# A fused attention and two-expert-layer kernel: dense chunks in the order 0, 6, 1, 7, …, sums of the output weights made in the dense blocks, and loads, splits and fetches of the output stage begun elsewhere

## The chip, the core and the metric

The kernel runs on one core of one Trainium2 chip. The metric is the device time of one launch in microseconds (us), taken as the median of several runs. All traces come from one profiled execution each.

## What is computed

Three layers follow one another; each works on the result of the one before. The reference, cut to its arithmetic:

```python
# attention: batch 4, 8 heads, 576 positions, 64 features, local mask or strided mask by head
x = softmax(mask(q @ k.T / 8)) @ v                    # -> 2304 tokens x 512
# dense layer: w_gate, w_val are 512 x 1536, w_out is 1536 x 512
x = (1 / (1 + exp(-(x @ w_gate)))) * (x @ w_val) @ w_out
# routed layer: w1 is 8 x 512 x 1024, w2 is 8 x 1024 x 512
do = (x @ w_skip) > 0
e  = argmax(x[do] @ w_gate2);  g = softmax(...)[e]
x[do] += g * (relu(x[do] @ w1[e]) @ w2[e])
```

The precision asked for is that of float32. The kernel splits an operand into a high part (a cast on ScalarE, to the matmul's float32r type) and a low part (the operand minus the high part, on VectorE), and forms each product from three matmuls (lines 563 to 565: high by high, high by low, low by high).

## The kernel before

**Stages.** Attention takes 0 to 138 us of the profiled execution, the dense blocks (gate and value products) 138 to 398, the output stage (the product with w_out) 398 to 576, and the routed experts the rest.

**Dense blocks.** The 1536 hidden features are 12 chunks f of 128; the tokens are three pairs p of two tiles of 384. `Block(f, p)` computes gate and value of one chunk for one pair by a Strassen-Winograd scheme of seven products (A11, A12, A22, S1 to S4 by B11, B21, B22, T1 to T4). `period` interleaves a block with the end of the block before, 42 matmuls of 384 columns, about 7.28 us. A block passes four PSUM tiles: psA, psB, psC and psD; ScalarE copies psB to psC (line 602, `onto`) before the products S4·B22 and A22·T4 of the block before are added to it. ACT is in order, so a copy stands behind whatever cast was queued ahead of it.

**Hidden results.** The gated result of a block goes to DRAM (`gts`) in the form in which the output stage wants it: seven operands B11, B21, B22 and T1 to T4 again. A chunk of the first half ("low") writes plain tiles with SP's queue; a chunk of the second half ("high") adds its own onto T2, T3 and T4 with accumulating DMAs from POOL's queue, and writes B21 and B22. With chunks in the order 0 to 11, all accumulations lie in the second half of the dense stage.

**Output weights.** w_out arrives as pairs of 32-bit words and is converted on DVE (`convert`, jobs of `background`) into 128 x 512 floats, stored with one DMA a chunk (line 556) to `wos`. The output stage loads quarters of it, makes the sums S1 to S4 (`sums_w`, lines 972 to 975, 12 DVE instructions of 128x512), stores three of them (`wss`, POOL's queue) and loads them again (line 948, SP).

**Output stage.** It has NSTEP = 63 steps k, 21 for each pair p: products P1 (k = 0 to 2 of a pair), P2, P6, P7, P5, P4, P3, three steps each, one for each group g of two chunks. A step has 12 matmuls. It needs an operand tile xt[k] (loaded from `gts`, line 938 or 941, five steps ahead, split by ACT at line 958 and DVE at line 966 two or three steps ahead) and a weight tile (wtA… for A11, A12, A22; wtS… for the sums; loaded at lines 948 and 951, split by `w_halves`). `finish` takes a finished pair of sums out of PSUM, splits it, and hands it to `turn_back`, whose narrow matmuls (lines 1075 and 1076) turn the result back to token rows and make the router's scores beside it; they run in small pieces between the products.

**What sets the order.** Instructions stand on each engine's queue in the order in which the program is written: the step loop runs a table `side` of actions by step (`at(k, …)`), and a list `after_act` of DVE work that is to follow ACT's. SP's DMA queue is in order, too: a DMA whose tile is still read, or whose source is still written, holds all that stand behind it. Moreover a DMA of SP waits for the one eight places ahead of it, since a ring of eight semaphores serves them.

**Places that the change touches.** The end of the dense stage, where A11 and xt2 are loaded at the start of block (11, 1) and xt0, xt1 and A12_0 at the start of (11, 2), while A12_1, A12_2, xt3 and xt4 follow the dense stage; the first 20 steps (`w_loads`, `sums_w`); `finish` at the change from one pair to the next; and the last steps, in which `fetch_head` (line 1193) fetches rows of expert 0's tokens from `xs`, a DRAM table that a scatter fills just before.

Of the kernel before, what the change touches and what calls it, by code (L numbers as in the profile page):

```python
# [23 lines left out]
def kernel(  # L24
# [51 lines left out]
    NG = NC // 4  # L76

# [23 lines left out]
    wos = [[dram.tile([128, 2, DM], F32, name=f"wo{h}_{g}") for g in range(NG)] for h in range(2)]  # L101
    wss = {(nm, g): dram.tile([128, 2, 256], F32, name=f"ws{nm}_{g}") for nm in ("S1", "S3", "S4") for g in range(NG)}

# [336 lines left out]
    def fetch_w(f, nm):  # L440
        raw = raw_of[f, nm] = raw_w([128, 4, 128, 2], I32, f"w{nm}{f}")
        if nm == "o":
            src = moe_w_out.bitcast(I32)[128 * f:128 * f + 128, :]
            nc.sync.dma_start(raw.rearrange("p c n t -> p (c n t)"), src)
        else:
            src = (moe_w_gate if nm == "g" else moe_w_val).bitcast(I32)[:, 256 * f:256 * f + 256]
            nc.sync.dma_start(raw.rearrange("p c n t -> p c (n t)"), src.rearrange("(c p) f -> p c f", p=128))
# [98 lines left out]

    def out_weights(f, follow=None):
        box = []

        def dst():  # L550
            if not box:
                box.append(part_x(f"wof{f}").rearrange("p a n -> p (a n)")[:, 0:DM])
            return box[0]

        def store():
            nc.sync.dma_start(wos[f // (NC // 2)][f % (NC // 2) // 2][:, f % 2, :], box[0])
# [3 lines left out]
        wo_jobs[f] = convert(f, "o", dst, store)  # L560
# [10 lines left out]
    class Block:  # L571
# [39 lines left out]
        def put(self, op, t, add=False):  # L611
            dst = gts[self.p, op, self.f % (NC // 2) // 2][:, self.f % 2, :]
# [5 lines left out]
        def store(self, nm, by, i):  # L618
# [4 lines left out]
            x, y, low = self.tm[nm], self.tm[by], self.f < NC // 2  # L623
# [232 lines left out]

    raws_left = []
    for f in range(2, NC):
        raws_left += [(f, "g"), (f, "v")] + ([(f - 3, "o")] if f > 2 else [])
    raws_left += [(f, "o") for f in range(NC - 3, NC)]  # L860
    outs_of = {f: [f - 2] for f in range(2, NC)}
    outs_of[NC - 2].append(NC - 3)
    outs_of[NC - 1] = [NC - 2, NC - 1]
# [50 lines left out]
    sum2 = []  # L914
    wt = {nm: [] for _, nm, _, _ in PROD}
    WHERE = {"A11": (0, 0), "A21": (0, 1), "A12": (1, 0), "A22": (1, 1)}
# [26 lines left out]
    def load_w(nm, g, of=None):  # L943

        if len(wt[nm]) <= g:
            wt[nm].append(slab([128, 2, 2, 256], F32, f"wt{nm}{g}"))
        if of == nm and nm[0] == "S":
            nc.sync.dma_start(wt[nm][g][:, 1], wss[nm, g])
        elif of:
            h, d = WHERE[of]  # L950
# [787 lines left out]
```

## Time and profile before

| | us |
|---|---|
| median of 3 runs | 771.02 |
| the runs | 770.71, 771.02, 773.42 |
| the profiled execution, its own time | 772.05 |
| its span (first to last instruction) | 770.3 |
| TensorE (PE) busy in the span | 719.8 (93%) |
| VectorE (DVE) busy | 561.1 (73%) |
| ScalarE (ACT) busy | 453.3 (59%) |
| GpSimd (POOL) busy | 258.1 (34%) |
| DMA traffic | 160.15 MB, mean 208 GB/s |

The busy share of PE is not a measure of its speed: matmuls are pipelined, and at a lower granted clock the same matmul counts as longer busy time. What PE could save is read from the time between two of its matmuls against their number. The pace of full clock stands in the dense blocks, where PE is busy throughout.

### The profile page before, as it was taken

The page shows a single profiled execution, that of the slowest core. Times are in us where ns is not written, and L with a number is a line of the kernel's source. Part 1 is how long each engine was busy: PE and PEld are TensorE (multiplying, and loading weights), DVE is VectorE, ACT ScalarE, POOL GpSimd, SP SyncE. Part 2 cuts the span into 40 slices and gives each one's busy share as a digit, 9 for nine tenths or more (in the row PEclk, how much of TensorE's full clock was granted, in tenths as well). Part 3 has the DMA queues.
Part 4 walks back from the last instruction along what each step waited for, and adds up shares of the span by engine and source line. Part 5 has one row for each costly group of instructions (what it writes and reads, how often), then busy time and mean ns, then how long its engine had stood idle before and what let it go on. Part 6 is the DMA issues. An engine that isn't in the chain of part 4 may idle for free.

```text
span 770.3 us, 14529 instructions
## 1 busy us (share of the span) xinstructions
PE 719.8 (93%) x4783; PEld 671.5 (87%) x4785; DVE 561.1 (73%) x1234; ACT 453.3 (59%) x1206; POOL 258.1 (34%) x296
## 2 busy tenths in 40 slices
PE   8999989999999999999976898999988999999994
PEld 5766667999999999999975798999977899999992
DVE  4799997988898888889654765657756756666760
ACT  5888885755455555555432655546654476767740
POOL 6677875000000043333331100210305355555510
PEclk9999999999999999999987898999999999999998
DMA  9999511466666699999989894786737677778720
GB/s 195 235 215 207 135 33 48 157 216 231 212 221 211 231 215 224 214 222 213 230 193 373 312 361 137 250 249 241 271 106 266 207 228 226 234 228 249 239 69 14
DMA packets 136555, 160.15 MB, mean 208 GB/s; under 512 B 60271, under 2 KB 104815, under 8 KB 136473
## 3 DMA queue, kind: packets, MB, share of 16 engines
q1 hardware_dynamic: 121208, 134.25, 56.7%
q0 software_dynamic: 12496, 21.49, 13.3%
q10 hardware_dynamic: 2768, 3.41, 1.2%
q8 instruction: 40, 0.66, 0.3%
q14 instruction: 43, 0.34, 0.1%
HBM read 105.07 MB, written 59.65 MB: 214 GB/s over the span
## 4 chain that ended last, share of the span: by engine, by line
PE 70%; DMA 9%; DVE 8%; ACT 5%; issue 3%; POOL 3%; SPq 1%; POOLq 0%; DVEq 0%; ACTq 0%
PE psZ L1524 5%; PE psB L564 5%; PE psB L565 5%; PE psB L563 5%; PE psA L563 4%; PE psA L565 4%; PE psD L565 4%; PE psD L563 4%; PE psA L564 4%; PE psD L564 4%; PE psX L1460 3%; PE psY L1460 2%; DMA xt<-gB 2%; DMA wtA<-wo 2%; POOL sm L313 2%
## 5 line engine op out<-in xcount | busy, mean ns | idle before, releaser
L614 POOL DMA_DIRECT2D gT<-sC x36 | 31.7, 1026 | 193.2 <-DVE sC L628 192.9
L958 ACT CAST xt<-xt 128x768 fp32r<-128x768 f32 (+1 forms) x74 | 53.6, 742 | 35.5 <-DMA xt<-gB 18.6
L966 DVE TENSOR_TENSOR xt<-xt 128x768 fp32r<-128x768 f32 (+1 forms) x74 | 60.4, 832 | 15.9 <-ACT xt L958 15.8
L300 ACT ACTIVATE sm<-psX,mx 96x128 f32<-96x128 f32 (+2 forms) x176 | 62.2, 378 | 9.8 <-DVE mx L294 7.8
L313 POOL TENSOR_TENSOR sm<-sm,rs 96x384 f32<-96x384 f32 (+2 forms) x64 | 55.5, 885 | 31.0 <-DVE rs L307 18.1
L609 DVE TENSOR_TENSOR u<-psD,u 128x384 f32<-128x384 f32 x70 | 38.7, 553 | 26.8 <-PE psD L565 26.7
L565 PE MATMUL psA<-xhB,wl 128*128 128x384 f32 x140 | 47.0, 336 | 1.3 <-DVE wl L536 1.3
L565 PE MATMUL psD<-xhT,wl 128*128 128x384 f32 x140 | 47.3, 338 | 0.3 <-DVE wl L536 0.3
L563 PE MATMUL psD<-xhT,wh 128*128 128x384 f32 x140 | 47.2, 337 | 0.0
L564 PE MATMUL psD<-xlT,wh 128*128 128x384 f32 x140 | 47.1, 337 | 0.0
L563 PE MATMUL psB<-xhT,wh 128*128 128x384 f32 x140 | 46.9, 335 | 0.0
L564 PE MATMUL psA<-xlB,wh 128*128 128x384 f32 x140 | 46.8, 334 | 0.0
L565 PE MATMUL psB<-xhT,wl 128*128 128x384 f32 x140 | 46.8, 334 | 0.0
L563 PE MATMUL psA<-xhB,wh 128*128 128x384 f32 x140 | 46.8, 334 | 0.0
L564 PE MATMUL psB<-xlT,wh 128*128 128x384 f32 x140 | 46.8, 334 | 0.0
L564 PE MATMUL psB<-xt,wtS 128*128 128x384 f32 x108 | 39.2, 363 | 4.1 <-DVE xt L966 4.1
L563 PE MATMUL psB<-xt,wtS 128*128 128x384 f32 x108 | 39.2, 363 | 3.2 <-ACT xt L958 1.8
L602 ACT COPY psC<-psB 128x384 f32<-128x384 f32 x35 | 16.3, 466 | 43.1 <-PE psB L565 43.1
L595 ACT COPY u<-psB 128x384 f32<-128x384 f32 x70 | 34.0, 485 | 12.7 <-PE psB L565 12.0
L1505 POOL DMA_INDIRECT out_dram<-xg x16 | 15.3, 956 | 77.4 <-DVE xg L1504 66.4
L565 PE MATMUL psB<-xt,wtS 128*128 128x384 f32 x108 | 39.1, 362 | 1.9 <-DVE wtS L1277 1.9
L300 ACT ACTIVATION_READ_ACCUMULATOR sm<-psX,mx 96x1 f32 (+2 forms) x176 | 38.7, 220 | 0.0
(786 smaller groups left out, 2536.5 us busy)
## 6 DMA issues: line engine op xcount, KB each, us to landing
w1r<-in_moe_w_dram SPq DMA_DIRECT2D x28, 512.0 KB
w2r<-in_moe_w_dram SPq DMA_DIRECT2D x28, 512.0 KB
xt<-gT SPq DMA_DIRECT2D x30, 384.0 KB
gT<-u SPq DMA_DIRECT2D x54, 192.0 KB
xt<-gB SPq DMA_DIRECT2D x22, 384.0 KB
gT<-sC POOLq DMA_DIRECT2D x36, 192.0 KB
gB<-sA SPq DMA_DIRECT2D x33, 192.0 KB
wg<-in_moe_w_gate_dram SPq DMA_DIRECT2D x12, 512.0 KB
```

Source lines behind the costliest of these rows:

```text
L300: nc.scalar.activation(sm[:n, w, 0:c], src[:, w, :], AF.Exp, bias=mx[:n, w:w + 1], accum_out=sums[:n, h, w:w + 1])
L313: nc.gpsimd.tensor_tensor(x, x, rs[:n, h, 0:m].rearrange("p (w o) -> p w o", o=1).to_broadcast([n, m, c]), op=ALU.mult)
L563: nc.tensor.matmul(ps, lhsT=whi, rhs=xhi, start=start, stop=False, skip_group_check=skip)
L564: nc.tensor.matmul(ps, lhsT=whi, rhs=xlo, start=False, stop=False, skip_group_check=skip)
L565: nc.tensor.matmul(ps, lhsT=wlo, rhs=xhi, start=False, stop=stop, skip_group_check=skip)
L595: nc.scalar.copy(self.tm[nm], self.ps["B"])
L609: nc.vector.tensor_tensor(self.tm[nm], self.ps["D"], self.tm[nm], op=ALU.add)
L614: nc.gpsimd.dma_start(dst, t, accum_op=ALU.add)
L958: nc.scalar.copy(h.bitcast(F32R), l)
L966: nc.vector.tensor_tensor(l.bitcast(F32R), l, h, op=ALU.subtract)
L1460: nc.tensor.matmul(ph, lhsT=w[kk][0][:, fs], rhs=xk, start=(kk == 0), stop=(kk == KD - 1))
L1524: nc.tensor.matmul(py, lhsT=w2h, rhs=h, start=(f == 0), stop=(f == NF - 1))
```

## The change

The chunks of the dense stage are taken in the order 0, 6, 1, 7, …, so that every second chunk is a low one and every second a high one. When a high chunk's w_out is converted, both halves for the group are there: four more DVE jobs make S1 to S4 of the chunk pair in place (128x256 each, 24 instructions in all) and SP stores the seven ready tiles (42 stores of 128 KB, in place of 12 of 256 KB). `sums_w`, `w_loads` and the table `wss` are gone; the output stage loads ready tiles with `load_w`.

A11, xt2, xt0, xt1 and A12_0 are all loaded at the start of block (11, 1), and their splits are jobs from the start of (11, 2). Behind the dense stage POOL loads S2_2, and SP A12_1, A12_2, S2_0, xt3 and xt4. The later weight tiles are loaded four steps ahead.

`finish` is cut up: sums that are added first (line 1238) are added at once, their casts follow one step later and the low parts behind them; others have the casts at once and the low parts in `after_act`. In the last four steps its tiles come from the pool of the operand tiles. Pieces of `turn_back` move by one to two steps. `fetch_head` moves from SP's queue to POOL's, one step later, and the loads of expert 0's weights (`load_e0`) by up to two steps.

```diff
+    CHUNK = [i // 2 + NC // 2 * (i % 2) for i in range(NC)]
...
-            src = moe_w_out.bitcast(I32)[128 * f:128 * f + 128, :]
+            src = moe_w_out.bitcast(I32)[128 * CHUNK[f]:128 * CHUNK[f] + 128, :]
...
         def store():
-            nc.sync.dma_start(wos[f // (NC // 2)][f % (NC // 2) // 2][:, f % 2, :], box[0])
+            for nm, a in ((("A12", 0), ("A22", 256)) if f % 2 else (("A11", 0),)):
+                put(nm, box(f)[:, a:a + 256])
...
+        j = convert(f, "o", lambda: box(f)[:, 0:DM], store)
+        if f % 2:
+            def sums(nm):
+                low, high = boxes[f - 1], boxes[f]
+                a11, a21, s1 = (low[:, 256 * i:256 * i + 256] for i in range(3))
+                a12, a22, s2 = (high[:, 256 * i:256 * i + 256] for i in range(3))
+                sub = nc.vector.scalar_tensor_tensor
+                if nm == "S1":
+                    sub(s1, in0=a21, scalar=-1.0, in1=a22, op0=ALU.mult, op1=ALU.subtract)
+                    put(nm, s1)
...
+                if nm == "S4":
+                    nc.vector.tensor_tensor(a11, a12, s2, op=ALU.subtract)
+                    put(nm, a11)
+            for nm in ("S1", "S2", "S3", "S4"):
+                j = Job("D", 0.4, lambda nm=nm: sums(nm), [j])
+        wo_jobs[f] = j
...
-            x, y, low = self.tm[nm], self.tm[by], self.f < NC // 2
+            x, y, low = self.tm[nm], self.tm[by], self.f % 2 == 0
...
-        if (f, p) == (NC - 1, NP - 1):
+        if (f, p) == (NC - 1, 1):
             for i in outs_of[f]:
                 need(wo_jobs[i])
-            for n in range(2):
+            for g in range(NG):
+                load_w("A11", g)
+            for n in (2, 0, 1):
                 load_x(n)
-            load_w("A12", 0, "A12")
-        if (f, p) == (NC - 1, 1):
-            for g in range(NG):
-                load_w("A11", g, "A11")
-            load_x(2)
+            load_w("A12", 0)
...
-    def finish(u, a, sums, adds=None):
-        sh, sl = (raw_w([128, 2, UT], F32R, f"s{n}{u}{a}") for n in "hl")
+    def finish(u, a, sums, k, adds=None):
+        if k < NSTEP - 4:
+            sh, sl = (raw_w([128, 2, UT], F32R, f"s{n}{u}{a}") for n in "hl")
+        else:
+            both = slab2([128, 2, 2, UT], F32R, f"s{u}{a}")
+            sh, sl = both[:, 0], both[:, 1]
...
+        if adds:
+            for c in range(2):
+                nc.vector.tensor_tensor(adds[c], adds[c], sums[c], op=ALU.add)
+            at(k + 1, do(lambda: (highs(adds), after_act.append(lambda: lows(adds)))))
+        else:
+            highs(sums)
+            if k + 1 < NSTEP:
+                after_act.append(lambda: lows(sums))
+            else:
+                lows(sums)
...
+    load_w("S2", 2, eng=nc.gpsimd)
+    for nm, g in (("A12", 1), ("A12", 2), ("S2", 0)):
+        load_w(nm, g)
     load_x(3)
-    for g in (1, 2):
-        load_w("A12", g, "A12")
     load_x(4)
-    w_loads(0)
-    at(0, do(lambda: w_loads(1)))
-    at(1, do(lambda: w_loads(2)))
...
-        xg, ins = fetch(0, PARTS[:1])
+        xg, ins = fetch(0, PARTS[:1], eng=nc.gpsimd)
...
-    at(NSTEP - 9, do(fetch_head))
+    at(NSTEP - 8, do(fetch_head))
```

On SP's queue at the end of the dense stage (wtA11g are the tiles of A11, wtA12g of A12, wtS2g of S2, each by group g; xt00 and xt01 are the halves of xt0) these rows stand in a row before; the store of the last converted chunk, wo1_2, is amid them:

```order
L938 DMA xt20_5007<-gB11_02_73 128x384
L938 DMA xt21_5008<-gB11_02_73 128x384
L556 DMA wo1_2_139<-wof11_4965 128x512
L938 DMA xt00_5082<-gB11_00_71 128x384
L938 DMA xt01_5083<-gB11_00_71 128x384
L938 DMA xt10_5086<-gB11_01_72 128x384
L938 DMA xt11_5087<-gB11_01_72 128x384
L951 DMA wtA120_5090<-wo1_0_137 128x2x256
L941 DMA xt3_5229<-gB21_00_74 128x768
L951 DMA wtA121_5212<-wo1_1_138 128x2x256
L951 DMA wtA122_5213<-wo1_2_139 128x2x256
L941 DMA xt4_5233<-gB21_01_75 128x768
```

and these after:

```order
L967 DMA xt20_5069<-gB11_02_73 128x384
L967 DMA xt21_5070<-gB11_02_73 128x384
L967 DMA xt00_5073<-gB11_00_71 128x384
L967 DMA xt01_5074<-gB11_00_71 128x384
L967 DMA xt10_5077<-gB11_01_72 128x384
L967 DMA xt11_5078<-gB11_01_72 128x384
L977 DMA wtA120_5081<-wA12_0_137 128x512
L977 DMA wtA121_5273<-wA12_1_138 128x512
L977 DMA wtA122_5274<-wA12_2_139 128x512
L977 DMA wtS20_5275<-wS2_0_146 128x512
L970 DMA xt3_5293<-gB21_00_74 128x768
L970 DMA xt4_5295<-gB21_01_75 128x768
```

The store of the last weights has moved ahead of all these loads, A12 and S2_0 stand ahead of xt3, and xt4 stands right behind xt3.

On ACT at the same place (ACTIVATE is a gate; the last row, a copy to psC, is what the PE needs for the last products of the dense stage) these stand before:

```order
L602 COPY psB_5112<-psA_5092 128x384
L958 CAST xt20_5007<-xt20_5007 128x384
L958 CAST xt21_5008<-xt21_5008 128x384
L606 ACTIVATE sC_111_5132<-psC_5099 128x384
L595 COPY u2_112_5140<-psB_5112 128x384
L606 ACTIVATE sA_112_5152<-psA_5092 128x384
L958 CAST xt00_5082<-xt00_5082 128x384
L958 CAST xt01_5083<-xt01_5083 128x384
L958 CAST xt10_5086<-xt10_5086 128x384
L958 CAST xt11_5087<-xt11_5087 128x384
L958 CAST wtA120_5090<-wtA120_5090 128x512
L602 COPY psC_5175<-psB_5112 128x384
```

and after:

```order
L636 ACTIVATE sC_111_5185<-psC_5156 128x384
L984 CAST wtA112_5067<-wtA112_5067 128x512
L625 COPY u2_112_5195<-psB_5167 128x384
L984 CAST xt20_5069<-xt20_5069 128x384
L984 CAST xt21_5070<-xt21_5070 128x384
L636 ACTIVATE sA_112_5210<-psA_5149 128x384
L984 CAST xt00_5073<-xt00_5073 128x384
L984 CAST xt01_5074<-xt01_5074 128x384
L984 CAST xt10_5077<-xt10_5077 128x384
L984 CAST xt11_5078<-xt11_5078 128x384
L984 CAST wtA120_5081<-wtA120_5081 128x512
L632 COPY psC_5235<-psB_5167 128x384
```

The five casts right ahead of the last copy to psC are the same ones. Ahead of them the cast of A11's last tile has come in behind the gate sC, and the copy to psB has moved out above the rows shown.

On SP in the last steps of the output stage (xg00 is what fetch_head fetches, r07 a weight of expert 0), before:

```order
L941 DMA xt59_6799<-gT4_22_133 128x768
L1193 DMA xg00_6815<-xs_69 128x521
L1171 DMA r07_6821<-in_moe2_w2_dram 128x2x512
L941 DMA xt60_6823<-gB22_20_119 128x768
L941 DMA xt61_6841<-gB22_21_120 128x768
L941 DMA xt62_6866<-gB22_22_121 128x768
```

and after:

```order
L970 DMA xt59_6819<-gT4_22_133 128x768
L970 DMA xt60_6836<-gB22_20_119 128x768
L1181 DMA r07_6859<-in_moe2_w2_dram 128x2x512
L970 DMA xt61_6861<-gB22_21_120 128x768
L970 DMA xt62_6883<-gB22_22_121 128x768
```

The fetch is no longer on this queue, and r07 stands behind xt60.

## Rows read from the trace of the kernel before

**Rows 1.** The page's slices of a 40th of the span, in tenths: clock, DMA.

```profile
PEclk9999999999999999999987898999999999999998
DMA  9999511466666699999989894786737677778720
```

**Rows 2.** Windows: length, busy PE, PEld, DVE, ACT, POOL, granted clock, DMA share, GB/s.

```profile
200.00:260.00 60.00, 60.00 (x348) 60.00 (x347) 50.45 (x92) 31.29 (x61) 0.00 (x0) 1.00 0.65 221
300.00:360.00 60.00, 60.00 (x348) 60.00 (x347) 51.71 (x94) 33.19 (x65) 21.81 (x25) 1.00 0.98 219
404.00:432.00 28.00, 17.66 (x66) 15.21 (x65) 17.08 (x27) 11.23 (x19) 5.79 (x14) 0.76 1.05 375
404.00:464.00 60.00, 47.04 (x233) 44.27 (x232) 37.60 (x61) 30.25 (x55) 5.79 (x14) 0.85 0.99 347
396.00:468.00 72.00, 58.73 (x284) 55.64 (x283) 44.10 (x71) 33.18 (x60) 9.59 (x19) 0.83 0.90 305
576.00:596.00 20.00, 17.51 (x120) 15.46 (x119) 13.23 (x60) 9.92 (x27) 8.74 (x16) 0.91 0.71 241
```

**Rows 3.** PE's timeline around the output stage's start: start, duration, [idle before and releaser].

```profile
387.84 0.34 PE L565 MATMUL psB<-xhT,wl 128*128 128x384 f32 x1
393.40 0.69 PE L563 MATMUL psC<-xhB,wh 128*128 128x384 f32 x1 [5.22 <-ACT psC L602]
...
398.61 0.33 PE L565 MATMUL psA<-xt,wtA 128*128 128x384 f32 x1
...
455.97 0.23 PE L1075 MATMUL psY<-wri,sh 128*128 128x148 f32 x1
...
456.37 0.39 PE L563 MATMUL psB<-xt,wtS 128*128 128x384 f32 x1
...
464.32 0.69 PE L564 MATMUL psB<-xt,wtS 128*128 128x384 f32 x1 [2.90 <-DVE xt L966]
...
469.04 0.62 PE L563 MATMUL psA<-xt,wtA 128*128 128x384 f32 x1
```

**Rows 4.** ACT's timeline from the last gates of the dense stage on.

```profile
386.37 0.50 ACT L606 ACTIVATE sA<-psA 128x384 f32<-128x384 f32 x1
...
390.68 1.10 ACT L958 CAST xt<-xt 128x384 fp32r<-128x384 f32 x2 [0.37 <-DMA xt<-gB]
392.35 0.62 ACT L958 CAST wtA<-wtA 128x512 fp32r<-128x512 f32 x1 [0.56 <-DMA wtA<-wo]
392.88 0.47 ACT L602 COPY psC<-psB 128x384 f32<-128x384 f32 x1
...
406.45 0.83 ACT L958 CAST xt<-xt 128x768 fp32r<-128x768 f32 x1 [1.81 <-DMA xt<-gB]
```

**Rows 5.** SP's DMA queue at the end of the dense stage, in its timeline.

```profile
388.03 0.32 SPq L941 DMA_DIRECT2D xt<-gB  x1
...
398.92 0.60 SPq L941 DMA_DIRECT2D xt<-gB  x1
```

**Rows 6.** Waits of SP's queue, 340 to 480: in total, times, longest.

```profile
SPq L951 <- PE psD L565: 9.3, 1, 9.3
```

**Rows 7.** SP's DMA queue in the last steps of the output stage.

```profile
547.73 0.40 SPq L941 DMA_DIRECT2D xt<-gT  x1
558.69 0.32 SPq L1193 DMA_DIRECT2D xg<-xs  x1
```

**Rows 8.** PE's timeline over those steps, to the first matmul of expert 0.

```profile
560.13 0.39 PE L563 MATMUL psD<-xt,wtA 128*128 128x384 f32 x1
...
576.14 0.33 PE L1422 MATMUL psY<-xx,we00h 128*128 128x256 f32 x1
```

**Rows 9.** DVE's groups, 395 to 440: busy, mean ns | idle before.

```profile
L966 DVE TENSOR_TENSOR xt<-xt 128x768 fp32r<-128x768 f32 (+1 forms) x11 | 9.4, 880 | 8.2 <-ACT xt L958 8.2
L972 DVE SCALAR_TENSOR_TENSOR sum<-wtS,wtA 128x512 f32<-128x512 f32 x3 | 2.1, 685 | 3.8 <-DMA wtA<-wo 3.8
```

**Rows 10.** DVE's groups by shape in the dense blocks, 200 to 360.

```profile
L519 DVE TENSOR_TENSOR stage<-stage 128x256 f32<-128x256 f32 x15 | 6.3, 421 | 0.2
```

More of the change, by code (lines that the diff above doesn't have):

```diff
@@ L100 @@
            for p in range(NP) for nm in ("B11", "B21", "B22", "T1", "T2", "T3", "T4") for g in range(NG)}
-    wos = [[dram.tile([128, 2, DM], F32, name=f"wo{h}_{g}") for g in range(NG)] for h in range(2)]
-    wss = {(nm, g): dram.tile([128, 2, 256], F32, name=f"ws{nm}_{g}") for nm in ("S1", "S3", "S4") for g in range(NG)}
+    wos = {(nm, g): dram.tile([128, 2, 256], F32, name=f"w{nm}_{g}")
+           for nm in ("A11", "A12", "A22", "S1", "S2", "S3", "S4") for g in range(NG)}
     manual = tc.manual_schedule()
@@ L855 @@
     late = late_p.__enter__()
+    outs_of = {f: [f - 1] for f in range(2, NC - 1)}
+    outs_of[1], outs_of[2] = [], [0, 1]
+    outs_of[NC - 2].append(NC - 2)
+    outs_of[NC - 1] = [NC - 1]
     raws_left = []
     for f in range(2, NC):
[L859 to L863, printed above, removed]
+        raws_left += [(f, "g"), (f, "v")] + [(i, "o") for i in outs_of[f - 1]]
+    raws_left += [(NC - 1, "o")]
     def more_raw():
@@ L913 @@
     xt = {}
-    sum2 = []
-    wt = {nm: [] for _, nm, _, _ in PROD}
-    WHERE = {"A11": (0, 0), "A21": (0, 1), "A12": (1, 0), "A22": (1, 1)}
+    wt = {}
     def flat2(x):
@@ L1010 @@
                 rest0.pop()()
-            if (f, p, i) == (NC - 1, 1, 4):
-                for x in wt["A11"] + [xt[2]]:
+            if (f, p, i) == (NC - 1, NP - 1, 0):
+                for x in [wt["A11", g] for g in range(NG)] + [xt[2], xt[0], xt[1], wt["A12", 0]]:
                     split_job(x)
         prev = k
-    for x in (xt[0], xt[1], wt["A12"][0]):
-        split_job(x)
     for eng in "AD":
@@ L1187, with fetch @@
     PARTS = ((0, HEAD), (HEAD, SLOTS))
-    def fetch(e, parts=PARTS, xg=None):
+    def fetch(e, parts=PARTS, xg=None, eng=nc.sync):
         if xg is None:
@@ L1313 @@
         tb = [later(lambda u=ub, a=a: turn_back(u, a)) for a in range(2)]
-        for k in range(8 if p else 10, 11 if p else 13):
+        for k in range(8, 11):
             at(b + k, ta[0])
-        for k in range(16, 19):
+        for k in range(17, 20):
             at(b + k, tb[1])
-        for k, n in ((19, 1), (20, 2)) if last else ((20, 1), (21, 1), (22, 1)):
-            at(b + k, ta[1], n)
+        if last:
+            at(b + 20, ta[1], 4)
+        else:
+            for k in range(20, 23):
+                at(b + k, ta[1])
         if last:
@@ L1401 @@
                     run(gen, n)
-            after(p, name)
+            after(p, name, k)
     flush(after_act)
```

124 lines of the change are left out of this document (54 added, 70 removed).

## The prediction, made before the changed kernel ran

> **What bounds the kernel now.** I read the page's slices first [rows 1]: the granted clock is at its full level (2.4 GHz) nearly everywhere and falls in slices 21 to 25 alone, the last apart: 385 to 481 us, the start of the output stage. The DMA is near full in that stretch up to slice 24, and in the six slices ahead of it, where the clock holds. Then the windows by stage [rows 2]. In the dense blocks PE is busy 60.00 of 60 us, both in the first half (200 to 260) and in the second (300 to 360), though the DMA share is 0.65 in one and 0.98 in the other: there PE alone sets the time, at 348 matmuls in 60 us, 0.172 us each. From 396 to 468 PE is busy 58.73 of 72 us at a clock of 0.83, so here something else ends last. The timelines of PE [rows 3, 8] give the size, those of ACT and SP [rows 4 to 7] the cause.
>
> From the end of the last product before the first stall, 387.84 + 0.17 = 388.01, to the first matmul of the second pair, 469.04, 81.0 us pass [rows 3]. Needed are 12 matmuls that end the dense stage, 2 that open a bank and 21 steps of 12: 266 x 0.172 = 45.8 us, and 7 turn-back pieces of 456.37 − 455.97 = 0.40, 2.8 us: 48.6 in all. So 32.4 us are lost, in three parts.
>
> (a) 388.01 to 398.61: 10.60 us for 16 matmuls (2.75), 7.85 lost: 5.22 wait for the copy to psC, and the rest is half clock (1.2 GHz) behind it: 0.69 for the matmul after the wait beside 0.34 before [rows 3]. That copy stands on ACT behind casts whose operands came late by DMA (the last, wtA, ended at 392.97) [rows 4].
>
> (b) 398.61 to 456.37: 57.76 us for 214 matmuls and 5 pieces (38.8), 18.95 lost. The DMA engines moved 375 GB/s at a share of 1.05 from 404 to 432 [rows 2]: operand tiles come at the pace of the DMA, behind the reloads of weights and their sums.
>
> (c) 456.37 to 469.04: 12.67 us for 36 matmuls and 2 pieces (7.0), 5.7 lost: 2.90 wait for DVE's low part of an operand tile, queued behind what `finish` passes to and fro between ACT and DVE, and half clock behind it [rows 3].
>
> A fourth part lies at the end: (d) 560.13 to 576.14 is 16.0 us for 48 matmuls, 5 pieces and 0.4 us of transposes (10.7), 5.3 lost [rows 8]. SP issued nothing from 547.73 to 558.69, as the fetch of xg waited for the scatter, and xt60 to xt62 stood behind it [rows 7]. All four together: 32.4 + 5.3 = 37.7 us.
>
> **The change, part by part.** *The chunk order* moves half of the accumulating DMAs from the second half of the dense stage to the first. Nothing is added: the share should come out near the mean of 0.65 and 0.98, 0.82, throughout. As PE is busy throughout at either share [rows 2], this costs nothing by itself; it leaves the DMA more room at the end.
>
> *The sums in the dense blocks* add 24 DVE instructions of 128x256. The row of that shape has 0.421 us [rows 10], so 10.1 us of DVE over 260, four in each pair of chunks (43.7 us): 1.7 us. DVE is busy 51.71 of 60 us there [rows 2], 37.7 of 43.7; with the sums 39.4. The cover is 4.3 us for each pair; were it gone, a late DVE would delay blocks one for one. They also add 30 stores, of half the size, beside PE; S4 is written over A11 and so waits on DVE for A11's store, which was issued a chunk earlier. I take nothing for both; bounds 0 and 3 us. Out of the output stage go 12 DVE instructions of 0.685 us [rows 9], 8.2 us of an engine whose own low parts [rows 9] PE waits for.
>
> *The loads at the end of the dense stage* now issue at the start of block (11, 1), one block (7.28 us) earlier for xt0, xt1 and A12_0. They then land at about 385 instead of 392, ahead of the gate at 386.37. The same five casts still stand ahead of the copy to psC: 386.37 + 0.49, four at 0.55 and one at 0.62, the copy at 0.47 [rows 4], gives 390.2, where PE is ready at 388.0. So of (a) about 2.0 stays and 5.85 goes; bounds 0.7 (casts drawn earlier by the jobs) and 5.
>
> *The operand tiles behind it.* xt3 waits for the same matmul as before, 388.03, but xt4, which stood behind wtA121's wait of 9.3 us for the dense stage's last product [rows 6] and was issued at 398.92 [rows 5], now follows xt3 at once. Its load took 398.92 to 406.45, 7.5 us [rows 4, 5]: it lands at 396, and with 0.83 for the cast, 0.88 for the low part [rows 9] and 0.47 for the copy to psB ahead of it is ready at about 398, when P1 ends. I leave 2.5 us of stall here, bounds 0 and 8.
>
> *The transfers.* Before, 32 transfers of 262,144 bytes for output weights followed the dense stage (2 of A12, 12 reloads, 9 stores of sums, 9 loads of them). Now 17 are loaded, of which some three ahead of the end: 14, so 18 x 0.26 = 4.7 MB less. From 396 to 468 the core moved 305 GB/s [rows 2], 22.0 MB. Less 4.7, less 5 operand tiles of the second pair (0.39 MB each, 2.0), plus 0.4 for xt3 and about 1.0 for stores left over from the last blocks: 16.7 MB are needed for the first pair. At the 347 GB/s of 404 to 464 [rows 2] that is 48 us; from 388 on, 436, and 438 with the split. PE, with the stalls above, comes to its last three steps at 388.0 + 4.5 + 254 x 0.172 + 2.4 = 438.6. So the DMA and PE come out level: (b) keeps only the 2.5 already counted and gains 16.45. Of (c) I leave 1.5, bounds 0 and 5.7 (what it is now), as `finish` now lets a step pass before its casts; 4.2 gained.
>
> *The end.* The fetch of xg waits on POOL's queue now, with a few gathers and stores behind it and no operand tile. SP goes on, xt60 to xt62 are issued about 10 us earlier. Of (d) 0.5 stays: 4.8 gained. If the fetch is late instead, expert 0 waits; it is needed 16 us after its issue at 558.69.
>
> **The sum.** 5.85 + 16.45 + 4.2 + 4.8 = 31.3. Against the profiled execution's 772.05: 740.75; that one lies 1.03 over the median of the runs, 771.02. So **740**. Where nothing stays, it is 772.05 − 37.7 − 1.0 = 733, and about 1 us more could come where the clock is 0.91 at the start of expert 0 [rows 2]: 732 is the low end.
>
> **The rivals.** *The DMA still sets the first pair's products.* If the engines give the mean rate of 305 GB/s instead of 347 [rows 2], since tiles are requested as ring and slots come free, 16.7 MB take 54.8 us, 6.8 more, and the stall brings half clock with it, some 3 us as in (a): 750. For it: a share of 1.05 shows how near the limit is; against it: the low mean has the stretches in which SP was held.
>
> *The early loads are late all the same.* The accumulations of chunk 11 run just then, and SP's ring makes each load wait for the one eight back; then (a) stays whole and xt4 slips by 2 us: 748.
>
> *The end stays as it is.* Behind the row: SP issued nothing for 11 us because of one wait in order [rows 7], so freeing the queue should bring the tiles earlier; that is 4.8 of the sum. If instead the tiles' own transfer is what is late (they share the engines with POOL's traffic), (d) stays and the time is 744.8. The Trainium skill, "DMA: Bandwidth & Descriptors", section "Issuing engines are not separate DMA queues", speaks for this: issuing on several engines saves only the sequencer's time of issue, which it calls small. By that rule the move of the fetch would bring next to nothing; here the trace differs, since the 11 us were a wait and no work of issuing.
>
> *Slower: DVE becomes the bound of the dense blocks.* The four sums come in a bunch, behind the conversion and in order ahead of the blocks' own adds. It starts to cost where a pair's extra DVE time, waits for A11's store with it, goes over the cover of 4.3 us; each us over costs one in each of six pairs. To come out slower than before it must eat the 31.3 us, 5.2 us a pair, so some 9.5 us of DVE time a pair instead of 1.7: at 6 lost a pair 740 + 36 = 776. Against it: PE has not waited in those 60 us windows [rows 2], and A11's store is a chunk old.
>
> **How the numbers follow.** Main case 0.62 (740). DMA still binding 0.13 (750), early loads late 0.12 (748), end unchanged 0.08 (745), DVE bound 0.05 (776). The range 732 to 754 holds the first four with the bounds of (a) to (c), leaving out DVE and the far ends of several at once. What a measurement can tell from no change is about 0.5%, 3.9 us, so faster means under 767.2. The first four (0.95) lie there, less 0.02 for far ends of several terms at once; of the DVE case 0.01 ends within the bound and 0.04 above: faster 0.93, same 0.03, slower 0.04.
>
> **What would show it.** Right: PE's wait for psC at the dense stage's end is 2 us or less instead of 5.22; from 388 to the first matmul of the second pair 57 us pass, not 81; no gap of 11 us on SP's queue before xt60; full clock behind 560; DVE under 55 busy in 60 us of dense blocks with PE at 60.00. Wrong: PE under 59 there, or waits of ACT for operand tiles throughout the first pair, as now.

## The result

| | before | changed |
|---|---|---|
| median, us | 771.87 (4 runs) | 746.49 (4 runs) |
| the profiled execution | 772.05 | 746.60 |
| its span | 770.3 | 744.8 |
| PE busy | 719.8 (93%) | 708.6 (95%) |
| DMA traffic | 160.15 MB | 158.57 MB |

The ratio of the times is 0.9697, with a 95% interval of 0.9624 to 0.977: the changed kernel is faster. The forecast was 740, with a range of 732 to 754. By the spans of the profiled executions the gain is 25.5 us, where 31.3 were forecast. Three of the four places gave about what was forecast, for reasons that are only in part those of the forecast; the fourth, (a), gave almost nothing.

Six moments on PE's timeline cut the span into stretches that can be compared, one by one. Those of the changed kernel (start, duration, then the idle time before and its releaser) answer to [rows 3, 8]:

```profile
388.46 0.34 PE L595 MATMUL psB<-xhT,wl 128*128 128x384 f32 x1
393.00 0.69 PE L593 MATMUL psC<-xhB,wh 128*128 128x384 f32 x1 [4.21 <-ACT psC L632]
...
397.65 0.52 PE L593 MATMUL psA<-xt,wtA 128*128 128x384 f32 x1
...
446.60 0.39 PE L593 MATMUL psA<-xt,wtA 128*128 128x384 f32 x1
...
496.52 0.39 PE L593 MATMUL psA<-xt,wtA 128*128 128x384 f32 x1
...
548.18 0.33 PE L1438 MATMUL psY<-xx,we00h 128*128 128x256 f32 x1
...
731.14 0.62 PE L1514 MATMUL psZ<-we77h,h 128*80 128x512 f32 x2
```

Three of these moments were not among the rows of before; they are the first product of the output stage, the first of its third pair and the last matmul:

```profile
398.05 0.52 PE L563 MATMUL psA<-xt,wtA 128*128 128x384 f32 x1
...
519.68 0.39 PE L563 MATMUL psA<-xt,wtA 128*128 128x384 f32 x1
...
758.58 0.62 PE L1498 MATMUL psZ<-we77h,h 128*80 128x512 f32 x2
```

| stretch | before | changed | gained | forecast |
|---|---|---|---|---|
| start to the last product before the stall | 388.01 | 388.63 | −0.62 | 0 |
| from there to the first output product (a) | 10.04 | 9.02 | 1.02 | 5.85 |
| first pair (b, c) | 70.99 | 48.95 | 22.04 | 20.65 |
| second pair | 50.64 | 49.92 | 0.72 | 0 |
| third pair to the first matmul of expert 0 (d) | 56.46 | 51.66 | 4.80 | 4.8 |
| experts, to the last matmul | 182.44 | 182.96 | −0.52 | 0 |
| last matmul to the end of the span | 11.72 | 13.66 | −1.94 | 0 |
| sum | 770.3 | 744.8 | 25.5 | 31.3 |

The forecast cut (a) from (b) at 398.61, two matmuls later than the table, which moves 0.56 us of before from one row to the other.

The windows of the changed kernel (length, busy PE, PEld, DVE, ACT, POOL, granted clock, DMA share, GB/s) answer to [rows 2]; 380 to 400 stands beside the same window of before, which comes last:

```profile
200.00:260.00 60.00, 60.00 (x348) 59.97 (x347) 52.86 (x99) 32.57 (x63) 13.07 (x15) 1.00 0.90 239
300.00:360.00 60.00, 60.00 (x348) 60.00 (x348) 53.13 (x98) 33.13 (x65) 11.34 (x13) 1.00 0.86 218
380.00:400.00 20.00, 15.79 (x76) 15.47 (x75) 13.83 (x25) 10.84 (x23) 9.61 (x14) 0.83 1.07 319
404.00:464.00 60.00, 59.23 (x362) 58.34 (x361) 40.90 (x80) 39.49 (x74) 1.45 (x6) 1.00 0.89 298
```

```profile
380.00:400.00 20.00, 14.06 (x65) 13.12 (x65) 12.30 (x22) 9.08 (x19) 8.11 (x12) 0.83 0.86 223
```

PE is still busy 60 of 60 in the dense blocks, with a DMA share that is now near even, and from 404 to 464 it is busy 59.23 at full clock where it had 47.04 at 0.85. At the seam, 380 to 400, the clock is 0.83 as before, and the DMA engines are fuller than before, 1.07 against 0.86. ACT's timeline there answers to [rows 4]:

```profile
388.60 0.51 ACT L984 CAST xt<-xt 128x384 fp32r<-128x384 f32 x1 [0.79 <-DMA xt<-gB]
390.17 0.51 ACT L984 CAST xt<-xt 128x384 fp32r<-128x384 f32 x1 [1.06 <-DMA xt<-gB]
390.94 0.51 ACT L984 CAST xt<-xt 128x384 fp32r<-128x384 f32 x1 [0.26 <-DMA xt<-gB]
391.95 0.62 ACT L984 CAST wtA<-wtA 128x512 fp32r<-128x512 f32 x1 [0.50 <-DMA wtA<-wA]
392.48 0.47 ACT L632 COPY psC<-psB 128x384 f32<-128x384 f32 x1
...
398.07 0.83 ACT L984 CAST xt<-xt 128x768 fp32r<-128x768 f32 x1 [2.25 <-DMA xt<-gB]
```

The five casts still wait for their tiles, one after the other, and the copy to psC is still behind them: 392.48 instead of 392.88 before. That is the part of the forecast that failed; the experiments on it stand under "The seam".

### The profile page after: what moved, and what is told of

Read it like the earlier page. It is cut to its first block, busy times and chain, and to the rows that moved or that the text cites. A ratio compares the mean times of both kernels' runs of the same rounds, so it can differ in the third digit from the quotient of the medians.

```text
span 744.8 us, 14549 instructions
## 1 busy us (share of the span) xinstructions
PE 708.6 (95%) x4783; PEld 663.7 (89%) x4785; DVE 561.4 (75%) x1246; ACT 452.1 (61%) x1206; POOL 258.7 (35%) x289
## 2 busy tenths in 40 slices
DMA packets 136858, 158.57 MB, mean 213 GB/s; under 512 B 60511, under 2 KB 105823, under 8 KB 136777
## 3 DMA queue, kind: packets, MB, share of 16 engines
q10 hardware_dynamic: 2768, 3.41, 1.3%
## 5 line engine op out<-in xcount | busy, mean ns | idle before, releaser
L1119 POOL COPY row<-lm_all 128x8 f32<-128x8 f32 x18 | 6.9, 424 | 94.4 <-DVE lm_all L1115 94.4
L593 PE MATMUL psB<-xt,wtS 128*128 128x384 f32 x108 | 36.9, 341 | 0.0
L594 PE MATMUL psB<-xt,wtS 128*128 128x384 f32 x108 | 36.3, 336 | 0.6 <-DVE xt L992 0.6
```

Of the source, the lines that this page charges most:

```text
L593: nc.tensor.matmul(ps, lhsT=whi, rhs=xhi, start=start, stop=False, skip_group_check=skip)
L594: nc.tensor.matmul(ps, lhsT=whi, rhs=xlo, start=False, stop=False, skip_group_check=skip)
```

## The experiments

Every kernel but order_only is the changed kernel with the edit shown or described; the diffs are cut to the lines that matter, and "..." marks a cut. Since the times of single runs scatter by some us, the stretches of the profiled executions are compared; the median stands beside them.

### The bytes of the output weights

**traffic_back.**

```diff
+    pads = [dram.tile([128, 2, 256], F32, name=f"pad{i}") for i in range(18)]
+    WN = ("A11", "A12", "A22", "S1", "S2", "S3", "S4")
+    for i in range(18):
+        at(i * 2 // 5, do(lambda i=i: nc.sync.dma_start(pads[i], wos[WN[i % 7], i % NG])))
```

> The changed kernel with 18 needless copies of 256 KB, from the weights' tables to DRAM tiles nobody reads, on SP's queue in steps 0 to 6: the bytes that the change took out of this stretch, without the sums and without anyone who waits for them. Theory 1 (the stretch was bound by the bytes that its DMA engines move): 18 x 0.26 = 4.7 MB at 350 GB/s are 13.5 us, and as the engines are full until 440 in the changed kernel, 8 to 14 us come back in the first pair: 755 to 761. Theory 2 (the chain load, sum, store, reload held the split weights, the bytes did not matter): the first pair stays at 49 to 51 us and the time at 746 to 749.

Median 756.82. The first pair takes 58.26 us instead of 48.95; the other stretches stay within 0.5 us. PE's waits from 395 to 460, by what it waited for (in total, times, longest), are these, the two largest of nine:

```profile
PE psB L594 <- DVE xt L992: 1.6, 3, 0.7
PE psY L1085 <- ACT sh L1252: 1.3, 1, 1.3
```

In the changed kernel the like list, from 395 to 450, has two entries:

```profile
PE psB L594 <- DVE xt L992: 0.6, 1, 0.6
PE psB L595 <- DVE wtS L992: 0.2, 1, 0.2
```

The copies have no reader, so what they cost, 9.3 us, they cost as traffic on the engines and on SP's queue; the window from 400 to 440 has a share of 1.03 with them and 1.04 without. Theory 1 holds: the changed kernel stands at the limit of its DMA engines in this stretch, and as many bytes more give back 9.3 of the 22.0 us. That is not the whole of it: of the 22.0 the order of finish has 1.4 to 3.9 (next), and some 9 to 11 are left for what hung on the transfers before. That is the chain of load, sum, store and reload, and xt4, late behind the hold of SP's queue in [rows 6]. Neither was put back by itself, so this part is argued and not shown.

### finish, and the fetch of expert 0's rows

**finish_at_once.** The body of `finish` is that of before, its tiles where the change has them.

> The changed kernel with finish as before: add, cast and low part of each half at once, in turn on DVE and ACT (its tiles stay where the changed kernel has them). Theory 1 (the 2.90 us wait for a low part and the half clock behind it, at the change to the second pair, came from that order): PE waits 2 to 3 us there again, with half clock, at one or two places: 749 to 752. Theory 2 (that wait was a late tile, behind the full DMA, and went with the transfers): 746 to 747.5.

Median 749.93. The wait of [rows 3] is back, at the same place and nearly the same size:

```profile
446.74 0.54 PE L594 MATMUL psB<-xt,wtS 128*128 128x384 f32 x1 [2.85 <-DVE xt L992]
```

The first pair takes 52.82, 3.87 more; the last pair 51.94, only 0.28 more. From 442.53 to 445.81 DVE's rows are the adds and low parts of finish, with two waits of 0.58 for ACT's casts between them, and the low part that PE waits for starts behind them, at 445.73. Behind the wait, from 446 to 451, the granted clock is 0.66, and the DMA share is 0.01. Theory 1: part (c) came from the order of finish on ACT and DVE, not from a late transfer. Its size is less sure: in end_back (below), with the same finish, PE waits 1.48 at that place, the clock stays at 1.00, and the first pair takes 50.39, only 1.44 more.

**fetch_on_sp.**

```diff
-        xg, ins = fetch(0, PARTS[:1], eng=nc.gpsimd)
+        xg, ins = fetch(0, PARTS[:1])
...
-    at(NSTEP - 8, do(fetch_head))
+    at(NSTEP - 9, do(fetch_head))
```

> The changed kernel with the fetch of expert 0's rows back on SP's queue, one step earlier, as before. Theory 1 (the end gained because SP no longer waits for the scatter): SP shows a gap of some 10 us ahead of xt60, PE waits for operand tiles near the end of the output stage and 4 to 6 us come back: 750 to 752.5. Theory 2 (the queue of the issuing engine does not matter, the end gained by the other moves, such as the finish and the expert loads): 746 to 747.5.

Median 748.60. SP's queue in this kernel, and then in the changed one (answers to [rows 7]):

```profile
524.87 0.38 SPq L970 DMA_DIRECT2D xt<-gT  x1
532.09 0.32 SPq L1203 DMA_DIRECT2D xg<-xs  x1
532.50 0.38 SPq L970 DMA_DIRECT2D xt<-gB  x1
```

```profile
525.56 0.37 SPq L970 DMA_DIRECT2D xt<-gT  x1
526.08 0.32 SPq L970 DMA_DIRECT2D xt<-gB  x1
```

The hold of the queue is back, 7.2 us where before had 11.0, but the last pair takes only 53.59, 1.93 more. Both theories missed: the hold is real, and it explains less than half of the 4.8.

**end_back.** Both edits, the fetch on SP and finish at once, in one kernel.

> The changed kernel with both the fetch on SP and finish at once, as before. The last pair took 56.46 us before and 51.66 with the change; the fetch alone put back gave 53.59, finish alone 51.94. Theory 1 (each hides the other: with low parts queued behind finish, a late tile costs more): the last pair takes 55.5 to 57 and the time is 751 to 755. Theory 2 (they add, and the rest of the gain is from the moved loads of the expert's weights): the last pair takes 53.5 to 54.3.

Median 753.50. The last pair takes 55.82, 4.16 more than the changed kernel, where the edits alone gave 1.93 and 0.28. PE's longest wait there is this:

```profile
548.79 0.66 PE L1231 MATMUL psY<-ident,xg 128*128 128x128 f32 x4 [2.96 <-DVE lp L1088]
```

By its mark this is theory 1: each edit covers for the other. DVE's rows ahead of that wait are the adds and low parts of finish (from 544.42) and the low part of an operand tile (547.67), so a late tile and a finish in hand meet there; that this is why the two cost more together is argued from this order. So the 4.8 us cannot be shared out between the two, undoing one alone would have understated both, and the 0.64 that neither brings back belong to other moves, which were not tried.

### The order of the chunks

**order_only.** The kernel before, with the new order of chunks and the tables' indices that go with it.

```diff
+    CHUNK = [i // 2 + NC // 2 * (i % 2) for i in range(NC)]
...
-            x, y, low = self.tm[nm], self.tm[by], self.f < NC // 2
+            x, y, low = self.tm[nm], self.tm[by], self.f % 2 == 0
```

> The kernel before with the chunk order 0, 6, 1, 7, ... and nothing else of the change. Theory 1 (the order only spreads the accumulating DMAs, PE sets the dense stage either way): DMA share 0.8 to 0.9 throughout the dense blocks, their end within 0.7 us of 388.0, the output stage as before: 769.5 to 772.5. Theory 2 (with fewer accumulations the loads at the end of the dense stage come earlier): the wait of 5.22 us for psC shrinks to under 3 and 2 to 4 us are gained.

Median 768.88; the ratio to the kernel before is 0.9983, interval 0.9957 to 1.001, so no difference that these runs can tell. Windows of it beside [rows 2]:

```profile
200.00:260.00 60.00, 60.00 (x348) 60.00 (x348) 50.46 (x92) 31.63 (x62) 13.11 (x15) 1.00 0.83 218
300.00:360.00 60.00, 60.00 (x349) 60.00 (x347) 51.73 (x94) 32.93 (x64) 11.36 (x13) 1.00 0.85 221
```

The share is even, 0.83 and 0.85 for 0.65 and 0.98, and PE's 60 of 60 don't move. Theory 1, with a little of theory 2: in its one profile the wait for psC is 4.28 instead of 5.22, the first pair takes 68.24 instead of 70.99, and the last 1.6 more.

### The seam: why (a) stayed

**loads_back.** The loads of xt0, xt1 and A12_0 stand at the start of block (11, 2) again, their splits behind it.

> The changed kernel with the loads of xt0, xt1 and A12_0 at the start of block (11, 2) again, and their splits behind the block, as before. Theory 1 (SP and the full DMA set the landing, the earlier place gained next to nothing): the wait for psC is 4 to 6 us and the time 746 to 748. Theory 2 (the earlier place brought what the dense end gained, and without it A12 and S2 stand ahead of them): the wait grows to 7 us or more, 749 to 752.

Median 746.25. The wait for psC is 4.70 us, the stretch (a) 9.52 instead of 9.02, and p = 1 begins at 447.93 instead of 446.60. A place one block earlier in the program was worth 1.3 us at most, not 5.85: theory 1. SP's rows show why. These are those of the changed kernel, in which L560 stores the tiles of the last chunks' output weights, L977 loads A11 and then A12, and L967 loads xt2, xt0 and xt1:

```profile
377.23 0.39 SPq L560 DMA_DIRECT2D wS<-wof  x1
377.72 1.37 SPq L977 DMA_DIRECT2D wtA<-wA  x3
379.18 3.04 SPq L967 DMA_DIRECT2D xt<-gB  x6
382.27 2.99 SPq L977 DMA_DIRECT2D wtA<-wA  x3
```

And these are the same loads before: A11, then xt0 and xt1, then A12_0:

```profile
372.94 1.92 SPq L951 DMA_DIRECT2D wtA<-wo  x3
...
376.81 4.93 SPq L938 DMA_DIRECT2D xt<-gB  x4
382.12 0.53 SPq L951 DMA_DIRECT2D wtA<-wo  x1
```

The last tile of the five, A12_0, was issued at 382.12 before and at 382.27 in the changed kernel; xt0 and xt1 even later than before. Before, one store alone stood between xt2 and xt0 on SP's queue, as the rows under "The change" have it, so the place in the program was no hold. Now the loads stand behind the stores of the last weight tiles and sums, which wait for DVE; the last is issued at 377.23. In loads_back A12_0 is issued at 383.41, 6.05 us ahead of the end of the last product before the stall (389.46); in the changed kernel it was 6.36 us, and before 5.89. The new place moved the issue by less than half a microsecond. The engines would have had room one block earlier, as the windows of the changed kernel and then of before show:

```profile
366.00:374.00 8.00, 6.50 (x38) 6.30 (x37) 7.76 (x17) 3.85 (x8) 0.00 (x0) 1.00 0.47 169
```

```profile
366.00:374.00 8.00, 8.00 (x48) 8.00 (x47) 7.29 (x14) 4.55 (x10) 3.23 (x4) 1.00 0.98 187
```

No kernel had the loads issued there, so what that would have gained was not tried.

**copy_first.**

```diff
-                for x in [wt["A11", g] for g in range(NG)] + [xt[2], xt[0], xt[1], wt["A12", 0]]:
+                for x in [wt["A11", g] for g in range(NG)] + [xt[2]]:
...
-    for _ in period(None, prev):
-        pass
+    for i, _ in enumerate(period(None, prev)):
+        if i == 0:
+            for x in (xt[0], xt[1], wt["A12", 0]):
+                split_job(x)
+            for eng in "AD":
+                while queue[eng]:
+                    need(queue[eng][0])
```

> The changed kernel (746.5) with one edit: the splits of xt0, xt1 and A12_0 are made behind the first step of the last block's end, so that ACT's last copy to psC stands ahead of their five casts. Theory 1 (the copy is held by the casts in order, the tiles themselves are nearly there): the wait for psC falls from 4.21 us to under 0.5, the first product of the output stage starts at 391 to 393 instead of 397.65; part of it is given back at P2, whose tile xt3 lands at 398: 742.5 to 744.5. Theory 2 (the tiles' landing sets the end whatever stands on ACT): PE stops as long in P1 for xt0 and xt1, or in P2 for xt3, and the time stays at 745.5 to 747.

Median 744.78. The wait for psC is 0.61, but six matmuls later PE waits 3.14 for DVE's add on psD, which now stands behind the low parts of the same late tiles. (a) is 7.97, and the second pair (p = 1) begins at 445.90 instead of 446.60. Neither theory foresaw that wait, and the median lies between the two ranges; the stretches are nearer to theory 2.

**copy_and_add_first.** As copy_first, with `i == 2`.

> As copy_first, but the five splits come one step later still, so that DVE's add on psD (held for 3.14 us behind the low parts in copy_first) also stands ahead of them. Theory 1 (only the order on ACT and DVE held the last products of the dense stage): no wait over 0.7 us there, no half clock, first product of the output stage at 391 to 392.5; up to 3 us are given back at P2, as xt3 lands at 398 or so: p = 1 starts 4 to 6 us earlier than in the changed kernel (446.6), 741 to 743. Theory 2 (the tiles' landing sets the end): waits of P1 and P2 together come to the 4 us again, p = 1 starts within 1.5 us of 446.

Median 746.75. (a) falls to 4.39, and the first pair grows to 51.67: p = 1 begins at 445.45, where the changed kernel's two profiles have 446.60 and 446.33. PE's waits behind the dense stage:

```profile
393.32 0.61 PE L1407 MATMUL psB<-xt,wtA 128*128 128x384 f32 x2 [0.78 <-ACT sC L636]
402.06 0.44 PE L593 MATMUL psA<-xt,wtA 128*128 128x384 f32 x1 [1.86 <-ACT psB L1420]
```

The last of them is the start of P2, whose copy on ACT stands behind the casts of xt3 (398.84), of two tiles of A12 and of xt4. Theory 2, by the beginning of p = 1: PE arrives earlier and waits further on.

**no_accum_11.**

```diff
+            if add and self.f == NC - 1:
+                return
             if add:
                 nc.gpsimd.dma_start(dst, t, accum_op=ALU.add)
```

> The changed kernel without the accumulating DMAs of chunk 11 (its part of T2, T3 and T4 is left out of the sums, all three pairs). Theory 1 (the tiles of the first product come late because the DMA engines are full with those accumulations): DMA share at 380 to 400 falls from 1.07 to about 0.8, the wait for psC from 4.21 to 1 to 2 us, xt3 lands 2 to 4 us earlier, 2 to 4 us off the time. Theory 2 (SP issues them too late, at 377.7 to 385.5, behind the last stores and its ring): the wait stays at 3.5 to 4.5 us and the time within 1.5 us of the changed kernel's.

One run, 740.01; the kernel leaves chunk 11's part out of T2, T3 and T4. ACT's timeline at the seam, to be held against that of the changed kernel above:

```profile
387.38 1.74 ACT L986 CAST xt<-xt 128x384 fp32r<-128x384 f32 x4
389.03 0.62 ACT L986 CAST wtA<-wtA 128x512 fp32r<-128x512 f32 x1
389.55 0.48 ACT L632 COPY psC<-psB 128x384 f32<-128x384 f32 x1
...
393.54 0.83 ACT L986 CAST xt<-xt 128x768 fp32r<-128x768 f32 x1 [1.60 <-DMA xt<-gB]
```

None of the five casts waits for its tile, and the copy ends at 390.03: the forecast had 390.2 (the gate ended later than it assumed, 387.49 instead of 386.86, and the casts followed each other faster). SP issued these loads from 377.8 to 385.2, as in the changed kernel (377.7 to 385.3). The wait for psC is 1.20 and (a) 5.40, xt3 is cast 4.5 us earlier, and p = 1 begins at 442.42, 4.2 us earlier. Of the 6.6 us between the two profiled executions, 4.2 lie ahead of p = 1; the rest comes in the experts and behind them and is not the seam's. Theory 1, but for one number: the share was to fall to 0.8, and from 380 to 400 it is 0.98, with 347 GB/s instead of 319. The engines stay nearly full; they carry the tiles instead. So leaving these accumulations out, with their bytes, brings 4.2 us in this profile, but they are not why the change brought nothing: POOL issues the same ones before, too, from 377.46 to 390.9, and the wait from issue to cast of A12_0 is 10.2 us before and 9.7 in the changed kernel.

**dense_end_mended.** The splits are placed around the gate sC, behind the last copy to psC and the add on psD; all S2 tiles are loaded behind xt4; and chunk 10's w_out is converted one block later.

```diff
+    for i, _ in enumerate(period(None, prev)):
+        for x in {2: (xt[0],), 3: (xt[1], wt["A12", 0])}.get(i, ()):
+            split_job(x)
...
-    load_w("S2", 2, eng=nc.gpsimd)
-    for nm, g in (("A12", 1), ("A12", 2), ("S2", 0)):
+    for nm, g in (("A12", 1), ("A12", 2)):
         load_w(nm, g)
     load_x(3)
     load_x(4)
+    load_w("S2", 0)
...
+        if (f, p) == (NC - 2, 1):
+            out_weights(NC - 2, more_raw)
```

> The changed kernel with four edits: the splits of xt0, xt1 and A12_0 stand behind the last copy to psC, with the gate sC amid them (ACT) and behind the add on psD (DVE); all S2 tiles are loaded behind xt4; chunk 10's w_out is converted one block later, so that DVE does not wait for a store (the 1.50 us wait of PE at 367.7). Theory 1 (order on ACT, DVE and SP): no wait at 367, none over 0.7 at the dense stage's end, P2 starts without the 1.86 us wait of copy_and_add_first, as xt3 and xt4 land some 2 us earlier: from the dense stage's end to p = 1 53.5 to 55.5 us instead of 57.97, 739 to 742. Theory 2 (the landing of the tiles under a full DMA sets the end): 55.5 to 57 as in copy_and_add_first (56.06), 742 to 745.

Median 745.27, the changed kernel beside it 745.18. (a) is down to 3.34, without half clock, and 3.33 us are waited for at P2 instead. SP's queue tells why:

```profile
383.12 9.32 SPq L977 DMA_DIRECT2D wtA<-wA  x3
392.50 0.90 SPq L970 DMA_DIRECT2D xt<-gB  x2
```

The longest wait of SP's queue in that stretch, from the list of its waits (in total, times, longest):

```profile
SPq L977 <- PE psD L595: 7.8, 1, 7.8
```

A load of A12 on SP stands for 7.8 us on PE's last product on psD, with xt3 and xt4 behind it. Before, A12_1 stood in the same way for 9.3 us [rows 6]. In the changed kernel and in put_off (below), where S2_2 is loaded on POOL's queue ahead of it, SP has no such wait. My reading is that the first load of a weight tile behind the dense stage carries the wait for the engines that still use the room; what exactly the wait guards the traces don't show. So this kernel doesn't tell the two theories apart by its time, though the stall moved as theory 2 has it. The third edit did nothing either: PE waits 1.54 at 367.48, as in the changed kernel (1.50).

**changed_again.**

> The changed kernel once more, beside the mended one on the same chip. By its first runs 746 to 747 (one of four was 755); each theory expects the same stretches as there: 9.0 us from the dense stage's end to the first product, 49 to p = 1, 51.7 in the last pair, and 13.7 behind the last matmul.

Median 745.18. The stretches: (a) 7.95, first pair 48.58, last pair 51.66, behind the last matmul 14.02. The last product before the stall ends 1.17 later than in the first profile, at 389.80 against 388.63, and the first output product all the same at 397.75 beside 397.65: its time is set by the tiles, not by PE. Gains of a us in (a) alone are therefore no result, and the beginning of p = 1 is the better mark.

**put_off.** The splits as in dense_end_mended, S2_2 on POOL again, S2_0 behind xt4, and POOL's stores of block (11, 1) behind those of (11, 2).

```diff
-            if add:
+            if (self.f, self.p) == (NC - 1, 1):
+                put_off.append(lambda: nc.gpsimd.dma_start(dst, t, **({"accum_op": ALU.add} if add else {})))
+            elif add:
...
+    for put in put_off:
+        put()
```

> The changed kernel with three edits: the splits of xt0, xt1 and A12_0 behind the last copy to psC (as in dense_end_mended), S2_0 loaded behind xt4 (S2_2 stays on POOL's queue), and the five POOL stores of block (11, 1), three of them accumulating, put off behind those of block (11, 2). Theory 1 (the tiles come late since the accumulations of chunk 11 fill the DMA engines; what is not needed before the second pair can wait): xt3 is cast at 394 to 396 instead of 398.07, P2 waits under 1.5 us, from the dense stage's end to p = 1 52.5 to 55 us instead of 57.97 and 56.5 (changed_again): 740 to 743. Theory 2 (the bytes are only moved, and the first pair's other tiles pay): 55.5 to 57.5 us, 743.5 to 746.

Median 749.29, against 746.49 and 745.18 of the changed kernel. Neither theory holds. The seam is mended as theory 1 has it: (a) is 3.33, xt3 is cast at 395.42, and P1 and P2 run through without a wait. But the first pair takes 58.38. POOL's and ACT's timelines, and then PE's:

```profile
405.68 0.58 POOL L981 DMA_DIRECT2D wtS<-wS  x1 [1.59 <-DMA xt<-gT]
```

```profile
416.28 0.62 ACT L988 CAST wtS<-wtS 128x512 fp32r<-128x512 f32 x1 [13.73 <-DMA wtS<-wS]
```

```profile
417.68 0.69 PE L593 MATMUL psB<-xt,wtS 128*128 128x384 f32 x1 [7.76 <-ACT xt L988]
```

The five stores put off stand ahead of S2_2's load on POOL's queue. It is issued at 405.68 instead of 400.27, lands 10.6 us later under full engines, and ACT, in order, holds every operand tile behind that one cast. No version was found that beats the changed kernel clearly.

## Why the forecast was right, and where it was not

**Nearly right by size, by mechanisms that are shown in part: (b) and (c).** 20.65 forecast, 22.04 measured. The DMA and PE come out level, as worked out: from 400 to 440 the DMA share is 1.04 at 354 GB/s, and PE is busy 39.98 of 40 us. Two mechanisms are each shown by a kernel of their own: as many bytes more cost 9.3 us (traffic_back), and the old order of finish 3.87 or 1.44 (finish_at_once, end_back). The other 9 to 11 us were not tried by themselves; perhaps 2.75 of them belong to the order of the chunks (order_only). The forecast had the rest in the late operand tiles and the reloads; before, PE waited 3.04 and 3.41 us in P2, on the casts and low parts of operand tiles:

```profile
407.71 0.44 PE L563 MATMUL psA<-xt,wtA 128*128 128x384 f32 x1 [3.04 <-ACT psB L1399]
412.90 0.69 PE L564 MATMUL psA<-xt,wtA 128*128 128x384 f32 x1 [3.41 <-DVE xt L966]
```

Both waits are gone in the changed kernel. What I left as stall, 2.5 and 1.5, was too much: PE's waits in the whole first pair come to 0.75.

**Right by size, wrong by reason: (d).** 4.8 forecast and 4.80 measured, but the step put all of it down to SP's hold by the fetch. Alone, that is worth 1.93; it takes finish as well to bring 4.16 back. That the sizes meet is luck. The rival by which the end stays as it was is out, as the last pair did gain 4.80 and the hold, put back, costs 1.93 of it. The Trainium skill, "DMA: Bandwidth & Descriptors", section "Issuing engines are not separate DMA queues", says that issuing on several engines saves only the time of issue. The trace differs here: what the move to POOL's queue saved was a wait in order, 11.0 us before and 7.2 in fetch_on_sp.

**Wrong: (a).** 5.85 forecast, 1.02 measured. The step that failed is the issue: I took it that loads placed one block earlier in the program are issued one block, 7.28 us, earlier, and so land at 385 instead of 392. They were not issued earlier at all: A12_0 at 382.27 instead of 382.12. Before, SP's queue ran ahead of the blocks: xt0 was issued from 376.81 on, though its place is the start of block (11, 2), at about 380.7 by an estimate of 388.01 − 7.28. Now the queue comes to these loads behind the stores of the last weight tiles and sums, up to 377.23; the prediction had put the added stores at nothing, as they run beside PE. From issue to cast A12_0 then took 9.7 us, as before (10.2), under engines that were near full in 380 to 400 both times (0.86 and 1.07). The end of the step was good: with the tiles there, the copy ended at 390.03 (no_accum_11) where 390.2 was worked out. The rival of the late early loads had the outcome and gave 748, with a chance of 0.12. Of its two causes the accumulations do delay the tiles (no_accum_11), but they did so before as well; SP's queue is the one that is new, through its stores more than its ring. Its second half, that xt4 slips too, cost nothing: PE itself came to P2 late enough for it.

**Too small to see: the sums on DVE.** I took nothing, with bounds of 0 and 3 us. DVE is busy 52.86 and 53.13 in 60 us, under the 55 named, and PE waits for it at one place where it did not before, 1.50 us. The cause is not S4's wait for A11's store but the next wait in DVE's order: the conversion of the next w_out waits for the sums' stores, since it writes into their buffer. DVE's and PE's rows:

```profile
364.95 0.43 DVE L460 TENSOR_SCALAR wof<-wo 128x512 int32<-128x512 int32 x1 [1.89 <-DMA wS<-wof]
```

```profile
367.70 0.44 PE L593 MATMUL psD<-xhT,wh 128*128 128x384 f32 x1 [1.50 <-DVE u L639]
```

The kernel before had a wait of 0.72 for psC in the dense blocks, at 382.44, which is gone; on balance they end 0.62 later. Whether another buffer would take the wait away was not tried.

**Not foreseen: the end of the program.** From the last matmul to the end of the span it is 11.72 before and 11.80 in order_only, 13.66 in the changed kernel and 13.0 to 14.0 in all kernels made from it. The engines' rows there are the same, one add on DVE and one store on POOL. Where the 2 us are spent is open.

The account of the miss: 31.3 − 4.83 (a) + 1.39 (b, c) + 0.72 (second pair) − 0.62 (dense) − 0.52 (experts) − 1.94 (end) = 25.5.

## What to carry to other kernels

A place in the program is not a time. Before subtracting a shift of place from a landing time, read when the queue issued the load, and what stands ahead of it there: a queue that runs ahead of the matmuls gains nothing from an earlier place, and stores put ahead of the load take the gain away. Then read how long the tiles take from issue to landing, and what else moves in that window. Where an engine in order carries both the copy that PE waits for and casts that wait for DMA, putting the copy ahead only moves the wait to the next consumer, unless the tiles come earlier, too. When two edits cover one stretch, undo them together as well as one by one.

## What the runs showed that I had not expected

- 18 copies of 256 KB in the first pair cost 9.3 us, less than the 13.5 us that their 4.7 MB take at 350 GB/s. From 400 to 460 the core moved 350 GB/s with them and 305 without (shares of 0.97 and 0.90), so they first filled what room there was.
- A load of 256 KB took 10.6 us from issue to landing in put_off with the engines full.
- Which queue carries the first load of a weight tile behind the dense stage decides whether SP's queue is held: 9.3 us before and 7.8 us in dense_end_mended, where it was on SP, and no such wait in the changed kernel and in put_off, where it was on POOL.
- Half clock followed the long stalls of the seam, and not the short ones: the granted clock of 388 to 400 is 0.72 in the changed kernel after a wait of 4.21 us and in copy_first after one of 3.14, 0.86 in changed_again after 3.69, and 1.00 in dense_end_mended and in copy_and_add_first, whose waits there are 0.78 us at most.
